# Two MLPs behind a Fourier transform on one core: VectorE's passes over a group of weights in another order and in other stages

## The chip, the core and the metric

The kernel runs on one core of a Trainium2 chip. The metric is device time in microseconds (us) of one execution; the kernel before took 1014.62 us (median of 3 runs, 1012.75 to 1015.59). One further execution was profiled: it took 1011.64 us, and its trace spans 1009.5 us from the first instruction to the last.

## The reference

```python
X = np.fft.fft(x, axis=1); X = np.fft.fft(X, axis=2); x = X.real      # x: 2 x 3008 x 256
x = x.reshape(6016, 256)
h = x @ w_in;   r = np.maximum(h, 0.0); g = r * r;                    x = g @ w_out     # d_ff 2048
h = x @ w2_in;  g = h * (1.0 / (1.0 + np.exp(-1.702 * h)));           out = g @ w2_out  # d_ff 2048
```

The four weight matrices are float64. The kernel gets them as 32-bit words (low word, high word) and makes fp32 numbers of them itself.

## The kernel before, in words

**Two parts.** In the first part (to about 505 us of the trace) the core transforms x, runs the first MLP and, between its steps, prepares all the weights. In the second part it runs the second MLP. The change touches the first part alone.

**Steps.** The first MLP runs in 128 steps (the loop at L701), each for one of 8 blocks of up to 378 columns and one of 16 groups of 128 features. In a step TensorE (PE) does 6 matmuls into the two halves of a PSUM pair (`front1`, L468 to L470; the pool `psa` holds two pairs) and, for the step that lies four back, 12 matmuls into accumulators (`back`, L483, pool `psb`). VectorE (DVE) makes `p` (L727) from the first half of the pair and the two parts of `h` (L729, L730) from the second half: only then is the pair free for the next `front1` but one. ScalarE (ACT) does Relu, Square and a rounded copy `gh` (L736, L737, L739), GpSimd (POOL) the rest `gl` = h - gh (L76, called from L744). In the steps of the set `SV` VectorE does Relu and Square in one pass (L734), in those of `VSTEPS` it does `gl` too. When a block of accumulators is done, ScalarE and VectorE copy one half of it each to SBUF (L596).

**A group of weights.** There are 16 groups, named (MLP, in or out, number). Each is a tile of 128 x 2048 words. `narrow` (L162) makes 128 x 1024 fp32 numbers of it in six passes: *abs* on ScalarE (L169); *low*, the low word times a constant, on ScalarE (L172, L180) for the keys in the set `RA` and on VectorE (L182) for the others; and on VectorE *clamp* (L173, needs abs), *shift* (L174, needs clamp), *merge* (L183, needs low and the raw words) and *sum* (L185, needs shift and merge). Then `widen` or `widen_in` splits the numbers into a rounded part (ScalarE, L208, L254) and a rest (POOL or VectorE).

**Where the passes stand.** Groups (0,0,0) and (0,1,0) are prepared before and in the first steps. For the other 14 `staged` (L214) says how many items of the generator each step takes: with the key in `RA` 2, 2, 2 (abs and low; clamp and shift; merge and sum), else 1, 3, 2 (abs; clamp, shift and low; merge and sum). Six of them belong to the first MLP (all with low on ScalarE), the eight of the second MLP follow from step 55 on. `background` (L573) takes the items at the end of a step, and from step 18 on they are not issued before the step's last `h` and `gh` (L752, L753). Within these bounds the compiler's scheduler sets the final order on each engine; an engine runs its instructions in that order and waits where the next one is not ready.

Of the kernel before, what the change touches and what calls it, by code (L numbers as in the profile page):

```python
# [12 lines left out]
AF = mybir.ActivationFunctionType  # L13
ALU = mybir.AluOpType
# [13 lines left out]
TOP = float(np.array(0x47EFFFFE, np.uint32).view(np.float32))  # L28
LEAST = float(np.array(0x38000000, np.uint32).view(np.float32))
# [14 lines left out]

LOW = {(0, 0, 0): "V", (0, 0, 1): "V", (0, 0, 2): "G", (0, 0, 3): "G", (0, 1, 0): "G", (0, 1, 1): "G", (0, 1, 2): "G", (0, 1, 3): "V", (1, 0, 0): "G", (1, 0, 1): "G", (1, 0, 2): "G", (1, 0, 3): "G", (1, 1, 0): "G", (1, 1, 1): "G", (1, 1, 2): "G", (1, 1, 3): "V"}
VSTEPS = {44, 45, 50, 58, 61, 72, 75, 82, 93, 96, 107, 110}
RA = {(0, 0, 0), (0, 0, 1), (0, 0, 2), (0, 0, 3), (0, 1, 1), (0, 1, 2), (0, 1, 3), (1, 0, 1)}
EOG = {1, 2, 3}
SV = {49, 51, 59, 60, 66, 73, 74, 79, 80, 94, 95, 101, 108, 109, 115}
LOWE = {(0, 0): "V", (0, 1): "G", (0, 2): "V", (0, 3): "V", (1, 0): "V", (1, 1): "G", (1, 2): "G", (1, 3): "V"}  # L50
# [13 lines left out]
def spectral_two_mlps_kernel(  # L64
# [5 lines left out]
    V, A, G, T = nc.vector, nc.scalar, nc.gpsimd, nc.tensor  # L70

    def f32(ap):
        return ap.bitcast(F32)
# [88 lines left out]
    def narrow(raw, ue, key=None):  # L162

        r = raw.rearrange("p (n w) -> p n w", w=2)
        lw, hw = r[:, :, 0], r[:, :, 1]
        u = ue[:, 0]
        uu, eu = u.bitcast(U32), ue[:, 1].bitcast(U32)

        yield lambda: A.activation(out=u, in_=f32(hw), func=AF.Abs)  # L169
        early = key in RA and key != (0, 0, 0)  # L170
        if early:
            yield lambda: A.activation(out=eu, in_=lw, func=AF.Copy, scale=2.0 ** -29)  # L172
        yield lambda: V.tensor_scalar(out=u, in0=u, scalar1=LEAST, scalar2=TOP, op0=ALU.max, op1=ALU.min)  # L173
        yield lambda: V.tensor_scalar(out=uu, in0=uu, scalar1=3, scalar2=0x3FFFFFF8,  # L174
                                      op0=ALU.logical_shift_left, op1=ALU.bitwise_and)

        if early:
            pass
        elif key in RA:
            yield lambda: A.activation(out=eu, in_=lw, func=AF.Copy, scale=2.0 ** -29)  # L180
        else:
            yield lambda: V.tensor_scalar(out=eu, in0=lw, scalar1=2.0 ** -29, scalar2=None, op0=ALU.mult)  # L182
        yield lambda: V.scalar_tensor_tensor(out=eu, in0=hw, scalar=0xC0000000, in1=eu,  # L183
                                             op0=ALU.bitwise_and, op1=ALU.bitwise_or)
        yield lambda: V.tensor_tensor(out=uu, in0=uu, in1=eu, op=ALU.add)  # L185

    def temp(pool, tag="xt"):
# [4 lines left out]
    def widen(mlp, kind, g, temps, dest, then=None, tag="xt"):  # L192
        low = G if LOW[mlp, kind, g] == "G" else V
        raw = raws.pop((mlp, kind, g))
        ue = temp(temps, tag)
        yield from narrow(raw, ue, (mlp, kind, g))
        if then:
            then()
        w = dest.tile([P, 2, 1024], F32R, tag="w", name="w")
        o = ue[:, 0]  # L200
        if (mlp, kind) == (0, 0):

            o = ue[:, 1]
            a, c = ue[:, 0, 0:512], ue[:, 0, 512:1024]
            yield lambda: (G if g in EOG else V).tensor_tensor(out=o[:, 0:512], in0=a, in1=c, op=ALU.add)
            yield lambda: V.scalar_tensor_tensor(out=o[:, 512:1024], in0=a, scalar=mask, in1=c,
                                                 op0=ALU.mult, op1=ALU.subtract)
        yield lambda: A.copy(w[:, 0], o)  # L208
        yield lambda: sub(low, w[:, 1], o, w[:, 0])
        if mlp and (kind, g) in PARKED:  # L210
            park((mlp, kind, g), w)
        weights[mlp, kind, g] = w

    def staged(key, gen):  # L214

        mlp, kind, _ = key
        first = (2, 2, 2) if key in RA else (1, 3, 2)
        for k in first + ((1,) if kind else (4, 1, 2) if mlp else (2, 1)):
            yield lambda: run(gen, k)
        yield lambda: run(gen)  # L220
# [271 lines left out]
    def run(gen, n=1 << 30):  # L492
        for _ in range(n):
            item = next(gen, None)
            if item is None:
                return False
            item()
        return True
# [35 lines left out]
    def small_w():  # L534
        yield from narrow(w1n_raw, w1n_t)
# [7 lines left out]
    def at(name, job):  # L543
        i, rate, end = PLAN[name]
        plan.setdefault(i, []).append((name, rate, job))
        if end is not None:
# [4 lines left out]
    at("odd0", lambda: odd_k(0, xp, "x2", 36))  # L551
    at("conv", lambda: chain(*(
        staged((0, k, g), widen(0, k, g, xp, (winp, wq)[k], tag=("t", "x0")[k],
                                then=(lambda k=k, g=g: load_w(0, k, g + 1)) if g < 3 else None))
        for g in (1, 2, 3) for k in range(2))))
# [145 lines left out]
    for i in range(n):  # L701
# [19 lines left out]
        elif done:  # L721
# [6 lines left out]
                               in1=ps[:, 0, 0:wd], op0=ALU.mult, op1=ALU.add)  # L728
# [76 lines left out]
    with tc.manual_schedule():  # L805
        for u in range(units + 2):
# [41 lines left out]
            if here:  # L848
                if p == 7 and j < BLKS - 1:
                    run(stage_a(j + 1))  # L850
                if rest is not None and not run(rest, 3 if j else (0, 2, 2, 4, 4, 4, 4, 4)[p]):
# [8 lines left out]
                                in1=cd[:, :, 0:wd], op=ALU.add)  # L860
# [155 lines left out]
```

## Time and profile before

| | |
|---|---|
| runs | 1014.62 us median (1012.75 to 1015.59) |
| profiled execution | 1011.64 us, span 1009.5 us |
| TensorE busy | 974.7 us (97%) |
| VectorE busy | 817.7 us (81%) |
| ScalarE busy | 609.9 us (60%) |
| GpSimd busy | 366.7 us (36%) |

Busy time says how much an engine had to do, not what it waited for. For that one reads the waits (who was idle until whom) and, around one group of weights, the instructions in order of time on the engines that wait.

### The profile page before, as it was taken

How to read it: one execution, taken by the hardware profiler on the slowest of the kernel's cores; microseconds unless marked ns; L12 is line 12 of the kernel's file. 1: busy time of each engine (PE TensorE's matmuls, PEld its weight loads, DVE VectorE, ACT ScalarE, POOL GpSimd, SP SyncE). 2: the span in 40 equal slices, each digit the busy share in tenths (PEclk: the TensorE clock that was granted, in tenths of full speed). 3: DMA queues.
4: the chain of work that ended last, by engine and by line, in shares of the span. 5: the costliest groups of instructions: out<-in, count | busy, mean ns of one | idle time of the engine just before them, and what ended most of it. 6: DMA issues, size and time to landing. Idle time of an engine off the chain costs nothing.

```text
span 1009.5 us, 14240 instructions
## 1 busy us (share of the span) xinstructions
PE 974.7 (97%) x5582; PEld 943.8 (93%) x5582; DVE 817.7 (81%) x1089; ACT 609.9 (60%) x758; POOL 366.7 (36%) x219
## 2 busy tenths in 40 slices
PE   8889989999999998999899999999999999999998
PEld 8579988999988897998899999999999999999997
DVE  7996888886898688895679888888888788888874
ACT  2588877866766676778645554545545445554443
POOL 2367687544768357778413302002020020200000
PEclk9999999999999999999999999999999999999999
DMA  7641221300332021201631100000100000000000
GB/s 293 213 148 44 84 103 43 104 31 25 115 118 112 32 84 65 81 1 62 218 103 59 65 1 31 31 32 31 31 1 32 31 32 31 1 31 1 32 1 31
DMA packets 22914, 65.22 MB, mean 65 GB/s; under 512 B 1856, under 2 KB 14272, under 8 KB 19648
## 3 DMA queue, kind: packets, MB, share of 16 engines
q1 hardware_dynamic: 22848, 64.32, 17.9%
q8 instruction: 43, 0.70, 0.3%
q14 instruction: 23, 0.19, 0.1%
HBM read 43.13 MB, written 21.19 MB: 64 GB/s over the span
## 4 chain that ended last, share of the span: by engine, by line
PE 69%; DVE 15%; ACT 7%; issue 5%; POOL 3%; DMA 1%; SPq 0%; DVEq 0%; ACTq 0%; POOLq 0%
PE psb L796 25%; PE psc L780 23%; PE psb L483 12%; PE psa L367 2%; ACT h L736 2%; PE psa L468 2%; ACT h L737 2%; DVE p L727 2%; PE psa L470 2%; DVE h L729 2%; PE psa L469 2%; DVE h L730 2%; POOL gl L76 1%; ACT gh L739 1%; DVE gl L76 1%
## 5 line engine op out<-in xcount | busy, mean ns | idle before, releaser
L76 POOL TENSOR_TENSOR gl<-h,gh 128x752 fp32r<-128x752 f32 (+1 forms) x116 | 224.9, 1944 | 139.2 <-ACT gh L739 108.6
L483 PE MATMUL psb<-gh,w 128*128 128x376 f32 (+1 forms) x1024 | 240.4, 338 | 2.4 <-ACT o L596 1.4
L796 PE MATMUL psb<-gh,w 128*128 128x376 f32 (+1 forms) x1024 | 237.7, 334 | 0.0
L483 PEld LDWEIGHTS psb<-gh,w 128*128 128x128 f32 x1024 | 183.6, 190 | 4.3 <-ACT o L596 2.0
L796 PEld LDWEIGHTS psb<-gh,w 128*128 128x128 f32 x1024 | 182.9, 188 | 0.0
L736 ACT ACTIVATE h<-h 128x752 f32<-128x752 f32 (+1 forms) x113 | 93.9, 832 | 74.5 <-DVE h L730 73.4
L861 ACT ACTIVATE g<-c 128x1128 f32<-128x1128 f32 (+1 forms) x64 | 73.7, 1152 | 98.9 <-DVE c L859 98.9
L483 PE MATMUL psb<-gl,w 128*128 128x376 f32 (+1 forms) x512 | 131.3, 337 | 2.0 <-POOL gl L76 2.0
L796 PE MATMUL psb<-gl,w 128*128 128x376 f32 (+1 forms) x512 | 129.9, 335 | 0.4 <-DVE gl L76 0.3
L739 ACT CAST gh<-h 128x752 fp32r<-128x752 f32 (+1 forms) x128 | 105.0, 822 | 22.6 <-DVE h L734 17.2
L630 POOL TENSOR_TENSOR ue<-raw 128x376 f32<-128x376 f32 (+1 forms) x16 | 19.4, 1235 | 270.5 <-DVE ya L76 270.4
L76 DVE TENSOR_TENSOR gl<-g,gh 128x1504 fp32r<-128x1504 f32 (+1 forms) x64 | 113.5, 1773 | 1.6 <-ACT gh L841 1.6
L841 ACT CAST gh<-g 128x1504 fp32r<-128x1504 f32 (+1 forms) x64 | 93.0, 1454 | 33.8 <-DVE g L832 33.8
L468 PE MATMUL psa<-eo,w 128*128 128x376 f32 (+1 forms) x256 | 89.2, 349 | 13.6 <-DVE h L730 8.2
L727 DVE SCALAR_TENSOR_TENSOR p<-n,w1n_t,psa 128x376 f32<-128x376 f32 (+1 forms) x128 | 76.2, 599 | 31.8 <-PE psa L470 31.7
L737 ACT ACTIVATE h<-h 128x752 f32<-128x752 f32 (+1 forms) x113 | 94.0, 834 | 3.0
L483 PEld LDWEIGHTS psb<-gl,w 128*128 128x128 f32 x512 | 93.4, 190 | 2.4 <-POOL gl L76 2.3
L796 PEld LDWEIGHTS psb<-gl,w 128*128 128x128 f32 x512 | 92.1, 188 | 1.0 <-DVE gl L76 1.0
L832 DVE TENSOR_TENSOR g<-g,c 128x1128 f32<-128x1128 f32 (+1 forms) x64 | 89.5, 1399 | 1.2 <-ACT g L861 1.2
L858 DVE TENSOR_TENSOR g<-g,psc 128x376 f32<-128x376 f32 (+1 forms) x64 | 35.0, 546 | 67.7 <-ACT g L857 67.7
L469 PE MATMUL psa<-eo,w 128*128 128x376 f32 (+1 forms) x256 | 85.9, 336 | 0.0
L470 PE MATMUL psa<-eo,w 128*128 128x376 f32 (+1 forms) x256 | 85.5, 335 | 0.0
(139 smaller groups left out, 1619.9 us busy)
## 6 DMA issues: line engine op xcount, KB each, us to landing
ydram<-o SPq DMA_DIRECT2D x18, 376.0 KB, 2.8
xt<-in_x SPq DMA_DIRECT2D x5, 1024.0 KB, 7.2
cst<-in_dfts SPq DMA_DIRECT2D x8, 570.0 KB, 5.6
raw<-ydram SPq DMA_DIRECT2D x6, 752.0 KB, 4.7
out<-o SPq DMA_DIRECT2D x11, 376.0 KB, 3.1
raw<-in_w1i SPq DMA_DIRECT2D x4, 1024.0 KB, 4.9
raw<-in_w1o SPq DMA_DIRECT2D x4, 1024.0 KB, 6.2
raw<-in_w2i SPq DMA_DIRECT2D x4, 1024.0 KB, 4.9
```

The lines of the kernel that those rows point to most:

```text
L76: eng.tensor_tensor(out=o, in0=a, in1=f32(b), op=ALU.subtract)
L468: T.matmul(o, lhsT=w[:, 0, fs], rhs=t[:, par, 0, 0:wd], start=True, stop=False)
L469: T.matmul(o, lhsT=w[:, 0, fs], rhs=t[:, par, 1, 0:wd], start=False, stop=False)
L470: T.matmul(o, lhsT=w[:, 1, fs], rhs=t[:, par, 0, 0:wd], start=False, stop=True)
L483: T.matmul(acc[j][ec][:, s, 0:wd], lhsT=w[:, hl, e0:e0 + P], rhs=(gh, gl)[gi][:, s, 0:wd], start=(first and hl == 0 and gi == 0), stop=(la ...
L727: V.scalar_tensor_tensor(out=p[:, 0:wd], in0=e128[blocks[j]][:, 0:wd], scalar=w1n_t[:, 0, f:f + 1], in1=ps[:, 0, 0:wd], op0=ALU.mult, op1= ...
L736: A.activation(out=hv, in_=hv, func=AF.Relu)
L737: A.activation(out=hv, in_=hv, func=AF.Square)
L739: last_a = A.copy(gh[:, :, 0:wd], hv)
L780: T.matmul(bank, lhsT=w[:, hl, slot * P:(slot + 1) * P], rhs=t[:, yl, i], start=(first and hl == 0 and yl == 0), stop=(hl == 1), skip_grou ...
L796: T.matmul(o[:, s, 0:wd], lhsT=w[:, hl, e0:e0 + P], rhs=g[:, 2 * i + s, 0:wd], start=(f == 0 and hl == 0 and g is gh), stop=(f == 15 and h ...
L841: A.copy(gh[:, :, 0:pw], g[:, :, 0:pw])
```

## The change

The order of the passes and the stages change; no pass gets another size.

- Keys not in `RA` (and not (0,1,0)): the first stage is now abs, low, merge; the second clamp and shift; the third sum (3, 2, 1 for 1, 3, 2). VectorE's passes begin one step earlier.
- Keys in `RA`, except (0,0,0): still 2, 2, 2, but merge stands in the second stage and shift in the third.
- (0,0,0), (0,1,0) and the small array of weights keep their order (the set `FIRST`).
- (1,0,1) leaves `RA`: its low moves from ScalarE to VectorE.

```diff
-RA = {(0, 0, 0), (0, 0, 1), (0, 0, 2), (0, 0, 3), (0, 1, 1), (0, 1, 2), (0, 1, 3), (1, 0, 1)}
+RA = {(0, 0, 0), (0, 0, 1), (0, 0, 2), (0, 0, 3), (0, 1, 1), (0, 1, 2), (0, 1, 3)}
+FIRST = {(0, 0, 0), (0, 1, 0), None}
...
+        def clamp():
+            V.tensor_scalar(out=u, in0=u, scalar1=LEAST, scalar2=TOP, op0=ALU.max, op1=ALU.min)
+
+        def shift():
+            V.tensor_scalar(out=uu, in0=uu, scalar1=3, scalar2=0x3FFFFFF8,
+                            op0=ALU.logical_shift_left, op1=ALU.bitwise_and)
+
+
+        def low():
+            if key in RA:
+                A.activation(out=eu, in_=lw, func=AF.Copy, scale=2.0 ** -29)
+            else:
+                V.tensor_scalar(out=eu, in0=lw, scalar1=2.0 ** -29, scalar2=None, op0=ALU.mult)
+
+        def merge():
+            V.scalar_tensor_tensor(out=eu, in0=hw, scalar=0xC0000000, in1=eu, op0=ALU.bitwise_and, op1=ALU.bitwise_or)
+
         yield lambda: A.activation(out=u, in_=f32(hw), func=AF.Abs)
...
+        if key in FIRST:
+            yield from (clamp, shift, low, merge)
         elif key in RA:
...
+            yield from (low, clamp, merge, shift)
         else:
...
+            yield from (low, merge, clamp, shift)
         yield lambda: V.tensor_tensor(out=uu, in0=uu, in1=eu, op=ALU.add)
...
-        first = (2, 2, 2) if key in RA else (1, 3, 2)
+        first = (2, 2, 2) if key in RA else (3, 2, 1)
```

In the rows of the changed kernel line numbers are larger: clamp is L171, shift L174, low L182 (ScalarE: L180), merge L185, sum L194, and `p` and `h` are L736, L738 and L739. The names `ue` and `raw` are the numbers in work and the words of a group, `psa` halves of a PSUM pair.

VectorE's order around group (1,0,0), before:

```order
L727 SCALAR_TENSOR_TENSOR p_3648<-n_2301,w1n_t_125,psa_3627 128x376
L729 TENSOR_TENSOR h_3647<-p_3648,psa_3628 128x376
L730 TENSOR_TENSOR h_3647<-p_3648,psa_3628 128x376
L182 TENSOR_SCALAR ue_3625<-raw_2978 128x1024
L727 SCALAR_TENSOR_TENSOR p_3682<-n_2301,w1n_t_125,psa_3661 128x376
L173 TENSOR_SCALAR ue_3625<-ue_3625 128x1024
L729 TENSOR_TENSOR h_3681<-p_3682,psa_3662 128x376
L174 TENSOR_SCALAR ue_3625<-ue_3625 128x1024
L730 TENSOR_TENSOR h_3681<-p_3682,psa_3662 128x376
L183 SCALAR_TENSOR_TENSOR ue_3625<-raw_2978,ue_3625 128x1024
L727 SCALAR_TENSOR_TENSOR p_3715<-n_2301,w1n_t_125,psa_3694 128x376
L185 ISA ue_3625<-ue_3625 128x2048
```

The same engine and the same steps in the changed kernel:

```order
L182 TENSOR_SCALAR ue_3625<-raw_2978 128x1024
L736 SCALAR_TENSOR_TENSOR p_3650<-n_2301,w1n_t_125,psa_3629 128x376
L185 SCALAR_TENSOR_TENSOR ue_3625<-raw_2978,ue_3625 128x1024
L738 TENSOR_TENSOR h_3649<-p_3650,psa_3630 128x376
L739 TENSOR_TENSOR h_3649<-p_3650,psa_3630 128x376
L736 SCALAR_TENSOR_TENSOR p_3683<-n_2301,w1n_t_125,psa_3662 128x376
L171 TENSOR_SCALAR ue_3625<-ue_3625 128x1024
L738 TENSOR_TENSOR h_3682<-p_3683,psa_3663 128x376
L174 TENSOR_SCALAR ue_3625<-ue_3625 128x1024
L739 TENSOR_TENSOR h_3682<-p_3683,psa_3663 128x376
L194 ISA ue_3625<-ue_3625 128x2048
L736 SCALAR_TENSOR_TENSOR p_3715<-n_2301,w1n_t_125,psa_3694 128x376
```

Low and merge moved a step up, clamp and shift kept their step and sum stands alone behind the second `h` pair; the other groups of the second MLP move in the same way.

VectorE's order around group (0,1,3), where a block of accumulators (`psb_1083`) is copied to SBUF, before:

```order
L727 SCALAR_TENSOR_TENSOR p_1338<-n_316,w1n_t_125,psa_1329 128x378
L173 TENSOR_SCALAR ue_1286<-ue_1286 128x1024
L727 SCALAR_TENSOR_TENSOR p_1385<-n_316,w1n_t_125,psa_1350 128x378
L596 COPY o_1318<-psb_1083 128x2x376
L174 TENSOR_SCALAR ue_1286<-ue_1286 128x1024
L729 TENSOR_TENSOR h_1337<-p_1338,psa_1330 128x378
```

The same place in the changed kernel:

```order
L605 COPY o_1318<-psb_1083 128x2x376
L736 SCALAR_TENSOR_TENSOR p_1338<-n_316,w1n_t_125,psa_1329 128x378
L171 TENSOR_SCALAR ue_1286<-ue_1286 128x1024
L738 TENSOR_TENSOR h_1337<-p_1338,psa_1330 128x378
L185 SCALAR_TENSOR_TENSOR ue_1286<-raw_1050,ue_1286 128x1024
```

The copy of the accumulators now stands ahead of two `p` and of clamp.

TensorE's order at the same place, behind the `front1` matmuls into psa_1351, before:

```order
L468 MATMUL psa_1398<-eo_304,w_874 128x378
L469 MATMUL psa_1398<-eo_304,w_874 128x378
L470 MATMUL psa_1398<-eo_304,w_874 128x378
L468 MATMUL psa_1435<-eo_304,w_874 128x378
L483 MATMUL psb_1358<-gh_1215,w_729 128x378 x2
```

And in the changed kernel:

```order
L492 MATMUL psb_1358<-gh_1215,w_729 128x378 x2
L492 MATMUL psb_1358<-gl_1252,w_729 128x378 x2
L492 MATMUL psb_1358<-gh_1215,w_729 128x378 x2
L492 MATMUL psb_1359<-gh_1215,w_729 128x378 x2
L492 MATMUL psb_1359<-gl_1252,w_729 128x378 x2
```

Four matmuls of later steps, which stood ahead of the new accumulators, now stand behind them.

## Rows read from the trace of the kernel before

**Rows 1.** The page, busy time (share) and instructions by engine.

```profile
PE 974.7 (97%) x5582; PEld 943.8 (93%) x5582; DVE 817.7 (81%) x1089; ACT 609.9 (60%) x758; POOL 366.7 (36%) x219
```

**Rows 2.** Waits of TensorE, 250 to 460 us: total us, times, longest.

```profile
PE psa L468 <- DVE h L730: 7.8, 8, 2.5
PE psb L483 <- ACT o L596: 1.4, 1, 1.4
```

**Rows 3.** Waits of VectorE, 60 to 505 us.

```profile
DVE ue L173 <- ACT ue L169: 6.9, 6, 1.9
```

**Rows 4.** The five passes on VectorE, 60 to 505 us: ns min/median/max.

```profile
L182 DVE TENSOR_SCALAR ue<-raw x7: 685/687/2292, 246.7 to 444.7; 128x1024 uint32<-128x1024 uint32 x7
L173 DVE TENSOR_SCALAR ue<-ue x12: 680/1372/2311, 64.2 to 445.8; 128x1024 f32<-128x1024 f32 x12
L174 DVE TENSOR_SCALAR ue<-ue x12: 675/694/1849, 66.5 to 446.5; 128x1024 uint32<-128x1024 uint32 x12
L183 DVE SCALAR_TENSOR_TENSOR ue<-raw,ue x12: 1210/1426/2576, 68.1 to 448.8; 128x1024 uint32<-128x1024 uint32 x12
L185 DVE CUSTOM_DVE_ANT_0 ue<-ue x12: 1207/1214/2739, 69.7 to 450.8; 128x2048 uint16<-128x2048 uint16 x12
```

**Rows 5.** Order of time at group (1,0,1): start, length, engine, [idle before <- releaser].

```profile
414.31 0.60 DVE L727 SCALAR_TENSOR_TENSOR p<-n,w1n_t,psa 128x376 f32<-128x376 f32 x1 [0.95 <-PE psa L470]
417.43 0.61 DVE L727 SCALAR_TENSOR_TENSOR p<-n,w1n_t,psa 128x376 f32<-128x376 f32 x1 [1.37 <-PE psa L470]
```

**Rows 6.** Order of time at group (1,0,0), VectorE, GpSimd and TensorE.

```profile
372.52 1.43 DVE L173 TENSOR_SCALAR ue<-ue 128x1024 f32<-128x1024 f32 x1 [0.96 <-ACT ue L169]
375.07 1.81 POOL L76 TENSOR_TENSOR gl<-h,gh 128x752 fp32r<-128x752 f32 x1 [1.67 <-issue]
375.38 2.58 DVE L183 SCALAR_TENSOR_TENSOR ue<-raw,ue 128x1024 uint32<-128x1024 uint32 x1
378.25 1.81 POOL L76 TENSOR_TENSOR gl<-h,gh 128x752 fp32r<-128x752 f32 x1 [1.37 <-ACT gh L739]
378.40 2.74 DVE L185 CUSTOM_DVE_ANT_0 ue<-ue 128x2048 uint16<-128x2048 uint16 x1
382.11 0.44 PE L468 MATMUL psa<-eo,w 128*128 128x376 f32 x1 [2.48 <-DVE h L730]
```

**Rows 7.** Order of time at group (1,1,2).

```profile
270.57 1.82 POOL L76 TENSOR_TENSOR gl<-h,gh 128x752 fp32r<-128x752 f32 x1
275.06 1.39 DVE L173 TENSOR_SCALAR ue<-ue 128x1024 f32<-128x1024 f32 x1 [1.45 <-ACT ue L169]
277.61 1.82 POOL L76 TENSOR_TENSOR gl<-h,gh 128x756 fp32r<-128x756 f32 x1 [1.72 <-issue]
283.14 0.44 PE L468 MATMUL psa<-eo,w 128*128 128x378 f32 x1 [0.90 <-DVE h L730]
285.61 0.44 PE L468 MATMUL psa<-eo,w 128*128 128x378 f32 x1 [1.15 <-DVE h L730]
```

**Rows 8.** Order of time at group (1,1,0).

```profile
400.14 1.36 DVE L173 TENSOR_SCALAR ue<-ue 128x1024 f32<-128x1024 f32 x1 [1.46 <-ACT ue L169]
404.52 2.32 DVE L185 CUSTOM_DVE_ANT_0 ue<-ue 128x2048 uint16<-128x2048 uint16 x1
407.81 0.44 PE L468 MATMUL psa<-eo,w 128*128 128x376 f32 x1 [1.53 <-DVE h L730]
```

**Rows 9.** Order of time at group (0,1,3).

```profile
137.78 0.89 DVE L173 TENSOR_SCALAR ue<-ue 128x1024 f32<-128x1024 f32 x1 [1.93 <-ACT ue L169]
139.24 0.44 PE L468 MATMUL psa<-eo,w 128*128 128x378 f32 x1 [1.95 <-DVE p L727]
140.37 0.94 DVE L596 COPY o<-psb 128x752 f32<-128x752 f32 x1 [1.19 <-POOL gl L76]
141.46 0.83 PE L483 MATMUL psb<-gh,w 128*128 128x378 f32 x2 [0.63 <-DVE o L596]
```

**Rows 10.** Busy time by engine, granted clock of TensorE, DMA, 140 to 160 us.

```profile
140.00:160.00 20.00, 19.37 (x103) 19.08 (x102) 18.90 (x26) 15.53 (x21) 13.38 (x8) 0.91 0.42 144
```

More of the change, by code (lines that the diff above doesn't have):

```diff
@@ L167, in narrow @@
         uu, eu = u.bitcast(U32), ue[:, 1].bitcast(U32)
-        yield lambda: A.activation(out=u, in_=f32(hw), func=AF.Abs)
[L170 to L178, printed above, removed]
+        def clamp():
[10 more added lines that the diff above has]
+            V.scalar_tensor_tensor(out=eu, in0=hw, scalar=0xC0000000, in1=eu, op0=ALU.bitwise_and, op1=ALU.bitwise_or)
+        yield lambda: A.activation(out=u, in_=f32(hw), func=AF.Abs)
+        if key in FIRST:
+            yield from (clamp, shift, low, merge)
         elif key in RA:
-            yield lambda: A.activation(out=eu, in_=lw, func=AF.Copy, scale=2.0 ** -29)
+            yield from (low, clamp, merge, shift)
         else:
-            yield lambda: V.tensor_scalar(out=eu, in0=lw, scalar1=2.0 ** -29, scalar2=None, op0=ALU.mult)
-        yield lambda: V.scalar_tensor_tensor(out=eu, in0=hw, scalar=0xC0000000, in1=eu,
-                                             op0=ALU.bitwise_and, op1=ALU.bitwise_or)
+            yield from (low, merge, clamp, shift)
         yield lambda: V.tensor_tensor(out=uu, in0=uu, in1=eu, op=ALU.add)
```

## The prediction

> **What bounds the kernel now.** I read the page first: TensorE is busy for 97% of the span, VectorE for 81% [rows 1]. So a change to VectorE's order can give back only what TensorE waits for VectorE, and the waits come next. Between 250 and 460 us, where seven of the eight groups of the second MLP are prepared, TensorE waits 8 times and 7.8 us in all for an `h`, and 1.4 us for ScalarE's copy of accumulators [rows 2]. Then I asked what VectorE itself waits for between 60 and 505 us: for 6.9 us, in 6 places, it stands at clamp until ScalarE has made abs [rows 3]. Last I read the instructions in order of time around the groups where TensorE stops [rows 6 to 9]. There the reader is to see two things: the wait for abs ahead of clamp, and passes that take twice their shortest time when a `gl` of GpSimd is running.
>
> **How much VectorE may do in a step.** At 414.31 and 417.43 VectorE has caught up with TensorE; a step is then 3.12 us, of which it idles 1.37 [rows 5]. So about 1.4 us of passes fit into a step for nothing. The shortest times are 0.69 for low, 0.68 for clamp, 0.68 for shift, 1.21 for merge and 1.21 for sum [rows 4]. Before, groups with low on VectorE put 0 / 2.05 / 2.42 us into their three steps, which is 0.65 + 1.02 = 1.7 over the free time; the changed kernel puts 1.90 / 1.36 / 1.21, 0.5 over in the first step, most of it given back by the third. On paper that is 1.2 to 1.7 us less lateness a group, and abs has a step's time to be ready. But the lateness is not the wait: with two PSUM pairs TensorE stops only when VectorE is more than a step behind, and most groups never come so far. Hence I take the groups one by one.
>
> **(1,0,0)** costs TensorE 2.48 us [rows 6]. VectorE waits 0.96 for abs; then clamp takes 1.43, merge 2.58 and sum 2.74, that is 0.75 + 1.37 + 1.53 over their shortest times [rows 4, 6]. Merge ends at 377.96 and sum at 381.14, each 1.08 after a `gl` of GpSimd ends (376.88 and 380.06): they stood still until GpSimd was through. The new order takes away the 0.96 surely. The five passes still have to find gaps between GpSimd's operations of 1.81, one in each step, and sum is still the last of them. Bounds: all 2.48 goes, or nothing. Shifting the passes by a step should spare about one third of the 3.65 of standing still, some 0.5 net of where it is met again; 0.96 + 0.5 = 1.4 or 1.5; I take -1.4.
>
> **(1,1,2)** costs 0.90 + 1.15 = 2.05 [rows 7]. The 1.45 of waiting for abs goes, but low would now be issued, by my estimate, behind an `h` pair at about 271.3, in the middle of the `gl` that runs from 270.57 to 272.39, and stand still for about 1.1; and the sum, at about 278.8, meets the `gl` of 277.61 or its successor. The second stop comes from a pass of `SV` that lies between two `h` in both kernels. Bounds -2.05 and +0.5 (one more pass standing still than now); I take -0.6.
>
> **(1,1,0)** costs 1.53 [rows 8]: 1.46 of waiting for abs, and a sum of 2.32. The first goes, low and clamp are likely to meet a `gl`. Bounds -1.53 and +0.5; -1.0. The 1.4 for ScalarE's copy [rows 2] stays: abs is ahead of this copy in ScalarE's order both times.
>
> **(1,0,3) and (1,1,1)** share what is left, 7.8 - 2.05 - 2.48 - 1.53 = 1.7. Neither waits for abs: of the 6.9 us in 6 places [rows 3], 0.96 + 1.45 + 1.46 + 1.93 lie at the four groups of [rows 6 to 9], and the 1.1 left lies at (0,0,3) and (1,0,2). So only the spread helps, and the new pair low and merge delays an `h` of the step ahead. Bounds -1.7 and +1; -0.3.
>
> **(1,0,1)** gets a pass that it did not have on VectorE: low, 0.69 at its shortest and 2.29 at its longest [rows 4]; ScalarE loses the same pass. VectorE idles 0.95 and 1.37 in the two steps ahead [rows 5], which covers low and merge (1.90) if they are not stopped, and TensorE does not wait there now. Bounds 0 and +2; +0.4.
>
> **(0,1,3)** is the one place where TensorE's own order changes. Now VectorE stands 1.93 for abs, TensorE stops for 1.95, and 0.63 more for VectorE's copy of the accumulators, which waits for a `gl` until about 140.3 [rows 9]. In the new order this copy comes first on VectorE, ahead of two `p` and clamp, and can't end sooner, since the same `gl` holds its buffer: `p` and clamp, 0.6 + 0.9 + 0.6 done before it today, come after it, so VectorE leaves the place 1 to 2 us later. TensorE does not have the four `front1` matmuls to fill the time (4 x 0.17, 974.7 over 5582 [rows 1]); it does half of the new accumulators (six, about 1.0) and then waits until about 141.2. So one wait of some 3.4 stands in the place of 1.95 + 0.63 = 2.6 with 0.7 of work still to do, 0.2 won at the end of the wait. The half that it does early is done today as well. In 140 to 160 us the granted clock is 0.91 on the mean [rows 10], so part of that stretch ran at the lower level (1.2 GHz) behind these waits; a longer wait may lengthen it. Bounds -1.5 and +2.5; +0.4.
>
> **The rest.** The other five groups with low on ScalarE cause no wait of TensorE that I found; theirs goes from 0 / 1.36 / 2.42 to 0 / 1.89 / 1.89, the same over the free time; 0, hidden by the second PSUM pair, and up to +1 where clamp, still waiting for abs, now stands ahead of an `h`. (1,0,2) and (1,1,3) have no wait to lose. DMA: the raw words are free as soon as merge has run, a step earlier, which no one waits for. The second part has none of these passes.
>
> **Sum.** -1.4 - 0.6 - 1.0 - 0.3 + 0.4 + 0.4 = -2.5. Against the profiled execution, 1011.64, that is 1009.1; that one ran 3.0 under the median of the runs shown, so on their footing I predict 1014.6 - 2.5 = 1012.1.
>
> The Trainium skill, SBUF — State Buffer, section "Who interferes with whom", says that VectorE and GpSimd share a pair of ports under an exclusive lock, that a VectorE instruction in a 2-port mode or with two SBUF inputs takes it, and that the later of the two "fully blocks" until the other has ended. The trace agrees: merge and sum end 1.08 after GpSimd does [rows 6]. By that rule alone lying evenly is worth nothing where a pass falls on a `gl`, and this makes the second rival below.
>
> **Rivals.** First: the waits for an `h` go almost wholly, because each of them needs the last bit of lateness and every group loses 1.2 to 1.7. For it: abs and these very passes stand ahead of the three longest waits [rows 6 to 8]. Against it: the amount of passes is the same and sum stays in its step. It gives 2.48 + 2.05 + 1.53 + half of 1.7 = 6.9 less, with the two costs above 6.1 less: 1008.5.
>
> Second, the other side: low and merge, now issued directly behind an `h` pair and often ahead of a `p` and `h`, meet the running `gl` and stand still, so that VectorE enters clamp's step later than today. The price of one is up to 1.5 (2.74 - 1.21, rows 4 and 6). It decides once VectorE is already a step behind, so in (1,1,2), (1,0,0), (1,1,0) and (1,1,1): 4 x 1.5 = 6.0 against the waits for abs that go, 1.45 + 0.96 + 1.46 = 3.9; +2.1. With (1,0,1) at its worst +2.0 this gives +4.1: 1018.7; for it speaks that low has been stopped to 2.29 and merge to 2.58 already [rows 4], against it that GpSimd's `gl` comes with each step, so most collisions are only traded.
>
> Third: nothing visible. What is saved ahead of a group is met again at its `gl`, its `SV` pass or its copies, TensorE's waits move but keep their sum: 1014.6.
>
> **How the numbers follow.** Forecast (1010.9 to 1013.4) 0.42; first rival 0.23; third 0.19; second 0.16. A difference of 0.3%, 3.0 us, is about what a measurement of this kernel can tell from no change. Faster by more than that, under 1011.6: the first rival 0.23 and some two fifths of the forecast, 0.17; together 0.40. Slower, over 1017.7: 0.13 of the second. Same: the remaining 0.47. The range reaches from the first rival with a clock that stays up in (0,1,3), 1007.0, to a second rival that decides in three groups, 1016.8.
>
> **What would show it.** In the trace of the changed kernel: VectorE's wait for abs falls from 6.9 to about 2.5, left at groups with low on ScalarE alone; TensorE's wait for `h` in 250 to 460 us falls from 7.8 to about 4.5; at (0,1,3) one wait of 3 to 4 us for VectorE's copy; no wait of TensorE over 1 us at (1,0,1). I am wrong if the waits for `h` stay at 7 or more (then GpSimd's lock decides), if they fall under 2, or if (0,1,3) costs over 5.

## The result: 0.5% slower, and the profile after

The changed kernel takes 1018.87 us (median of 7 runs, 1016.65 to 1021.32), the kernel before beside it 1013.83 us; the ratio is 1.0053, 95% interval 1.0038 to 1.0067. I had forecast 1012.1 us, with a range up to 1016.8. The profiled execution took 1021.32 us, its span is 1019.4 us.

The page of the changed kernel, busy time by engine, answers to [rows 1]:

```profile
PE 986.7 (97%) x5582; PEld 954.0 (94%) x5582; DVE 820.2 (80%) x1090; ACT 610.4 (60%) x757; POOL 362.9 (36%) x219
```

VectorE has the same work (817.7 before). TensorE does the same 5582 matmuls in 12 us more; its mean granted clock was 0.984 in this execution and 0.996 in that of the kernel before, so part of the matmuls ran at the lower level.

TensorE's waits between 250 and 460 us, against [rows 2], and VectorE's wait for abs between 60 and 505 us, against [rows 3] (total us, times, longest):

```profile
PE psa L477 <- DVE p L736: 3.5, 4, 2.1
PE psa L477 <- DVE h L739: 2.3, 8, 0.3
```

```profile
DVE ue L171 <- ACT ue L187: 1.4, 3, 1.1
```

The wait for abs fell from 6.9 to 1.4 us, the wait for `h` from 7.8 to 2.3; but waits of 3.5 us for a `p`, which now stands behind low and merge, came in their place. The longest of them is at (1,1,0):

```profile
404.74 0.44 PE L477 MATMUL psa<-eo,w 128*128 128x376 f32 x1 [2.07 <-DVE p L736]
```

The ScalarE copy of [rows 2] (1.4 us at 400 us) is not gone either: TensorE waits for it a block later, 1.8 us at 462.

The five passes on VectorE, 60 to 505 us (ns min/median/max), against [rows 4]:

```profile
L171 DVE TENSOR_SCALAR ue<-ue x12: 678/804/2125, 63.7 to 451.4; 128x1024 f32<-128x1024 f32 x12
L185 DVE SCALAR_TENSOR_TENSOR ue<-raw,ue x12: 1210/1226/2850, 66.0 to 449.4; 128x1024 uint32<-128x1024 uint32 x12
L174 DVE TENSOR_SCALAR ue<-ue x12: 677/680/694, 68.0 to 453.3; 128x1024 uint32<-128x1024 uint32 x12
L194 DVE CUSTOM_DVE_ANT_0 ue<-ue x12: 1210/2228/2850, 69.1 to 454.8; 128x2048 uint16<-128x2048 uint16 x12
L182 DVE TENSOR_SCALAR ue<-raw x8: 686/1346/2156, 249.2 to 448.3; 128x1024 uint32<-128x1024 uint32 x8
```

Clamp and shift are short now (median 1372 to 804 and 694 to 680, the longest shift 1849 to 694), but sum takes 2228 where it took 1214, and low 1346 where it took 687. The standing still has moved from two passes to two others: the seven long sums all end about 1 us after a `gl` of GpSimd does.

The end of each block of accumulators gives marks for the comparison. VectorE's copies of three of them, the last one just behind the start of the second part, in the kernel before (start, length; `...` stands for rows left out):

```profile
222.07 0.94 DVE L596 COPY o<-psb 128x752 f32<-128x752 f32 x1
...
455.47 0.93 DVE L596 COPY o<-psb 128x752 f32<-128x752 f32 x1
513.86 0.93 DVE L802 COPY o<-psb 128x752 f32<-128x752 f32 x1
```

The changed kernel:

```profile
227.21 0.94 DVE L605 COPY o<-psb 128x752 f32<-128x752 f32 x1
...
461.26 0.93 DVE L605 COPY o<-psb 128x752 f32<-128x752 f32 x1
524.93 0.94 DVE L811 COPY o<-psb 128x752 f32<-128x752 f32 x1
```

From the first row to the second, where the second MLP's groups are prepared and where I had looked for the effect, it is 233.4 us before and 234.1 after. Yet TensorE waits 3.9 us less there: between 250 and 460 us 9.7 us before (7.8 + 1.4 [rows 2], and 0.5 in two short waits), 5.8 after. The stretch between these two copies (length; busy time of PE, PEld, VectorE, ScalarE, GpSimd; clock; DMA), before and after:

```profile
222.07:455.47 233.40, 223.76 (x1265) 211.70 (x1263) 192.60 (x276) 163.25 (x211) 150.15 (x92) 1.00 0.20 72
227.21:461.26 234.05, 227.61 (x1264) 214.50 (x1262) 194.11 (x277) 163.06 (x210) 146.19 (x92) 0.99 0.20 71
```

What the waits gave back went into the matmuls: TensorE is busy for 3.85 us more, with the same matmuls (1265 and 1264 records). Part of it may be the clock: the granted clock is 0.91 in 280 to 300 and in 400 to 420 us, in both traces of the changed kernel, and 1.00 in this trace of before. How much of the 3.85 us that makes was not separated.

In these two traces the loss lies on either side of the stretch: 5.1 us ahead of 227 us, and 5.3 us at the end of the first part (58.4 against 63.7). The second traces, below, make both smaller.

### The profile page after: what moved, and what is told of

Same layout as the page of the kernel before. It is cut to its first block, busy times and chain, and to the rows that moved or that the text cites. A ratio compares the mean times of both kernels' runs of the same rounds, so it can differ in the third digit from the quotient of the medians.

```text
span 1019.4 us, 14237 instructions
## 1 busy us (share of the span) xinstructions
PE 986.7 (97%) x5582; PEld 954.0 (94%) x5582; DVE 820.2 (80%) x1090; ACT 610.4 (60%) x757; POOL 362.9 (36%) x219
## 4 chain that ended last, share of the span: by engine, by line
PE 62%; DVE 12%; ACT 4%; issue 2%; POOL 0%; DVEq 0%; ACTq 0%; POOLq 0%
PE psb L805 25%; PE psc L789 23%; PE psb L492 9%; DVE p L736 2%; DVE h L738 2%; PE psa L376 2%; DVE h L739 2%; PE psa L477 1%; DVE ue L194 1%; DVE h L743 1%; PE psa L479 1%; PE psa L478 1%; ACT h L746 1%; ACT h L745 1%; DVE gl L77 1%
## 5 line engine op out<-in xcount | busy, mean ns | idle before, releaser
L77 POOL TENSOR_TENSOR gl<-h,gh 128x752 fp32r<-128x752 f32 (+1 forms) x116 | 221.6, 1918 | 151.1 <-ACT gh L748 118.1
L492 PEld LDWEIGHTS psb<-gh,w 128*128 128x128 f32 x1024 | 187.6, 194 | 6.0 <-DVE o L605 3.4
L805 PEld LDWEIGHTS psb<-gh,w 128*128 128x128 f32 x1024 | 182.9, 188 | 0.0
L77 DVE TENSOR_TENSOR gl<-g,gh 128x1504 fp32r<-128x1504 f32 (+1 forms) x64 | 111.4, 1740 | 1.6 <-ACT gh L850 1.6
L477 PE MATMUL psa<-eo,w 128*128 128x376 f32 (+1 forms) x256 | 90.0, 352 | 11.2 <-DVE h L739 4.8
L736 DVE SCALAR_TENSOR_TENSOR p<-n,w1n_t,psa 128x376 f32<-128x376 f32 (+1 forms) x128 | 76.2, 599 | 28.2 <-PE psa L479 28.1
L492 PEld LDWEIGHTS psb<-gl,w 128*128 128x128 f32 x512 | 95.6, 194 | 0.4 <-POOL gl L77 0.4
L805 PEld LDWEIGHTS psb<-gl,w 128*128 128x128 f32 x512 | 92.1, 188 | 1.0 <-DVE gl L77 1.0
L738 DVE TENSOR_TENSOR h<-p,psa 128x376 f32<-128x376 f32 (+1 forms) x128 | 69.7, 544 | 21.1 <-POOL gl L77 8.2
L478 PE MATMUL psa<-eo,w 128*128 128x376 f32 (+1 forms) x256 | 86.3, 338 | 0.0
```

The costliest lines, as they stand in the source:

```text
L77: eng.tensor_tensor(out=o, in0=a, in1=f32(b), op=ALU.subtract)
L477: T.matmul(o, lhsT=w[:, 0, fs], rhs=t[:, par, 0, 0:wd], start=True, stop=False)
L478: T.matmul(o, lhsT=w[:, 0, fs], rhs=t[:, par, 1, 0:wd], start=False, stop=False)
L492: T.matmul(acc[j][ec][:, s, 0:wd], lhsT=w[:, hl, e0:e0 + P], rhs=(gh, gl)[gi][:, s, 0:wd], start=(first and hl == 0 and gi == 0), stop=(la ...
L736: V.scalar_tensor_tensor(out=p[:, 0:wd], in0=e128[blocks[j]][:, 0:wd], scalar=w1n_t[:, 0, f:f + 1], in1=ps[:, 0, 0:wd], op0=ALU.mult, op1= ...
L738: V.tensor_tensor(out=h[:, 0, 0:wd], in0=p[:, 0:wd], in1=ps[:, 1, 0:wd], op=ALU.add)
```

## The experiments

The table has the median of each kernel, its difference from the median of the kernel before in the same comparison, and the ratio with its 95% interval. The ratio differs from the quotient of the medians by up to 0.1% (1 us), so a difference of medians is known no better than that. Three kernels were traced once more: before (1016.04 us), the changed kernel (1021.93) and ra_no_012 (1013.39).

| kernel | us | difference | ratio, 95% |
|---|---|---|---|
| w2_only | 1013.79 | 0.0 | 0.9998 (0.9982 to 1.0013) |
| w2_and_101 | 1014.23 | +0.5 | 1.0009 (0.9993 to 1.0025) |
| ra_only | 1018.83 | +5.1 | 1.0046 (1.0031 to 1.0062) |
| old_012 | 1016.71 | +3.0 | 1.0031 (1.0017 to 1.0046) |
| only_012 | 1015.36 | +1.5 | 1.0010 (0.9995 to 1.0024) |
| ra_no_012 | 1017.00 | +3.2 | 1.0023 (1.0009 to 1.0038) |
| only_101 | 1014.84 | +1.5 | 1.0012 (1.0000 to 1.0023) |
| mlp1_no_012 | 1013.43 | +0.1 | 1.0005 (0.9993 to 1.0017) |
| new_001 | 1016.91 | +3.1 | 1.0020 (1.0002 to 1.0037) |
| w2_222 | 1019.66 | +6.0 | 1.0057 (1.0039 to 1.0074) |
| nyq_before | 1013.42 | -0.3 | 0.9989 (0.9975 to 1.0003) |
| after_yb | 1016.04 | +2.7 | 1.0031 (1.0019 to 1.0042) |
| before_yb | 1012.47 | -1.0 | 0.9989 (0.9978 to 1.0000) |
| before_nyq_yb | 1011.98 | -1.4 | 0.9985 (0.9974 to 0.9996) |
| w2_nyq_yb | 1011.23 | -2.2 | 0.9978 (0.9965 to 0.9991) |

**Which part of the change.** *w2_only* is the changed kernel with both edits on `RA` undone, *w2_and_101* with the second alone:

```diff
-RA = {..., (0, 1, 3)}
+RA = {..., (0, 1, 3), (1, 0, 1)}
-            yield from (low, clamp, merge, shift)
+            yield from (low, clamp, shift, merge)
```

*ra_only* keeps that order line, has (1,0,1) in `RA`, and undoes the staging:

```diff
-            yield from (low, merge, clamp, shift)
+            yield from (clamp, shift, low, merge)
-        first = (2, 2, 2) if key in RA else (3, 2, 1)
+        first = (2, 2, 2) if key in RA else (1, 3, 2)
```

> Only the groups of the second MLP are staged 3, 2, 1; the groups with low on ScalarE keep their old order, (1,0,1) too. Theory 1 (the time is lost at the first MLP's groups, where the copy of the accumulators at (0,1,3) now comes first and TensorE waits once for long): within 2 us of the kernel before, since the waits for h that go (about 4 us less between 250 and 460) are mostly met again. Theory 2 (low and merge of the second MLP's groups meet GpSimd): 3 to 5 us slower than before. Theory 3 (the waits keep their sum and what is lost is the clock, which falls after them more often): slower by half of the time that the granted clock is low beyond the kernel before's.

> The changed kernel, but with the old order (shift ahead of merge) in all groups with low on ScalarE; the second MLP's groups are staged 3, 2, 1 and (1,0,1) has low on VectorE. Theory 1: 4 to 5 us faster than the changed kernel, about as before. Theory 2: as the changed kernel, 5 us slower than before. Theory 3: by its low clock, as in the run with the second MLP's groups alone.

> Only merge and shift change places in the groups with low on ScalarE ((1,0,1) is still one of them); the second MLP's groups keep 1, 3, 2. Theory 1: 4 to 5 us slower than before, with the long wait for the copy at (0,1,3). Theory 2: within 1 us of before. Theory 3: slower by half of the additional time at the low clock, wherever that lies.

The staging by itself gives nothing and loses nothing that the interval can tell (-1.8 to +1.3 us); merge ahead of shift in the groups with low on ScalarE loses 5.1 us by itself. ra_only turns (1,0,1) too, which the change does not. The change's own order edit is what lies between w2_and_101 and the changed kernel: 1.0009 to 1.0053, about 4.5 us, with intervals that do not overlap. So by edits the change is 0.0 for the staging, 0.5 for (1,0,1) (not beyond its interval) and 4.5 for the order of six groups of the first MLP. Theory 2 falls; theory 3, the clock, is not excluded as a part of it. w2_only does gain where I forecast it, and gives it back at the end of the first part. Its copies at the same three places:

```profile
225.75 0.94 DVE L605 COPY o<-psb 128x752 f32<-128x752 f32 x1
...
457.43 0.93 DVE L605 COPY o<-psb 128x752 f32<-128x752 f32 x1
519.56 0.93 DVE L811 COPY o<-psb 128x752 f32<-128x752 f32 x1
```

231.7 us in the middle (233.4 before), then 62.1 (58.4 before). Of the 1.7 us won, 1.4 is the wait for ScalarE's copy, which has only moved behind the second row.

**Which group.** *old_012* is the changed kernel, but (0,1,2) keeps shift ahead of merge; *only_012* the kernel before with (0,1,2) alone reordered; *ra_no_012*, *mlp1_no_012* and *only_101* are ra_only with the new order in a part of the groups; *new_001* is w2_and_101 with the new order in (0,0,1) alone. The line of old_012 and ra_no_012:

```diff
-            yield from (low, clamp, merge, shift)
+            yield from (low, clamp, *((shift, merge) if key == (0, 1, 2) else (merge, shift)))
```

> The changed kernel, but group (0,1,2) alone with shift ahead of merge: by that alone the scheduler gives TensorE, and the copy of the accumulators at (0,1,3), the order of the kernel before again. Theory 1: 3 to 5 us faster than the changed kernel. Theory 2: no difference from the changed kernel (under 1 us). Theory 3: a difference only if the low clock of 125 to 205 us goes with it, about 3 us.

> The kernel before, with merge ahead of shift in group (0,1,2) alone; by that the scheduler turns the copy of the accumulators at (0,1,3) and TensorE's four matmuls there into the order of the changed kernel. Theory 1 (this turned order is the whole loss): 4 to 5 us slower than before. Theory 2 (it is a part of it, as taking it back gave 2.2 us, and the rest lies in the other groups with low on ScalarE): 2 to 3 us slower.

> Merge ahead of shift in all groups with low on ScalarE but (0,1,2); the second MLP's groups as before, TensorE's order as before. Theory 1: within 1 us of before, or up to 2 us faster since TensorE's wait at 51 us gets shorter. Theory 2: 2.5 to 3 us slower than before.

> The kernel before with merge ahead of shift in (0,0,1), (0,0,2), (0,0,3), (0,1,1) and (0,1,3), not in (0,1,2) and (1,0,1). If the first MLP's groups carry the loss of 2 to 3 us: as slow as that kernel; if (1,0,1) does: within 1 us of before.

> The kernel before with merge ahead of shift in group (1,0,1) alone. The kernel without (0,1,2) but with the other groups with low on ScalarE reordered lost 2 to 3 us, and its traces differ from before's only behind 380 us. If (1,0,1) carries that loss: 2 to 3 us slower than before. If the first MLP's groups carry it: within 1 us of before.

> The second MLP's groups staged 3, 2, 1, (1,0,1) with low on VectorE, and of the groups with low on ScalarE (0,0,1) alone with merge ahead of shift, so that merge runs before the h pair and TensorE's wait at 51 us (2.5 us before, 0.3 in the changed kernel) gets shorter; TensorE's order as before. Theory 1: 1 to 2 us faster than the kernel before, the sum of this wait and of what the second MLP's groups give. Theory 2: 0 to 3 us slower, if the order of (0,0,1) is where the rest of the loss comes from.

The copy at (0,1,3) that comes first there is made so by the order of *another* group, (0,1,2): old_012 gives TensorE the old order and 2.2 us (1.0053 to 1.0031, with intervals that overlap a little; ra_only to ra_no_012, the same step without the staging, is 1.8). Alone it costs 1.5 us, an amount that its interval does not tell from nothing, so theory 1 is a part at most. (1,0,1) alone (only_101) costs 1.5 more, at the edge of its interval, the other five groups of the first MLP nothing that shows. These parts make 3.1 of ra_only's 5.1; each is known to some 1.5 us, and whether the rest is error or comes of their combination stays open. The same question stands in the changed kernel: old_012 differs from w2_and_101 by the new order of these five groups alone and is 2.5 us slower, where mlp1_no_012 has the same five without the staging and loses 0.1; the two intervals overlap. new_001 is a miss: the wait at 51 us stayed at 1.97 us, and its 3.1 us loss (by the ratio 2.0, just beyond its interval) is not explained by (0,0,1), since mlp1_no_012 has the same edit and does not lose.

TensorE's wait at (0,1,3) in only_012, and the stretch of [rows 10] in it:

```profile
141.73 1.00 PE L492 MATMUL psb<-gh,w 128*128 128x378 f32 x2 [3.87 <-DVE o L605]
```

```profile
140.00:160.00 20.00, 18.27 (x90) 18.27 (x91) 17.39 (x27) 13.82 (x18) 12.41 (x7) 0.83 0.37 125
```

One wait of 3.87 us in the place of 1.95 + 0.63 [rows 9], as forecast; behind it the granted clock of the stretch is 0.83, not 0.91, so twice as much of it ran at 1.2 GHz, and the pair of matmuls behind the wait takes 1.00 where it took 0.83 [rows 9]. This clock is not firm: the second trace of before has 1.00 in 140 to 160 us, and both traces of the changed kernel have 0.91.

**Two traces of one program.** *before_2*, *after_2* and *ra_no_012_2* are unchanged kernels, traced again.

> The kernel before once more, for a second trace of it: its first one was at 1011.64 us 2 us faster than the median of its runs and had a mean granted clock of 0.996 where most of its runs have 0.990. If the difference between the two shown traces is the clock's, this one shows as much low clock as the changed kernel's trace and waits about as long in all; if not, the clock stays near 0.996.

> Another trace of the changed kernel, whose first one was of its slowest run. What belongs to the change must show again: the wait of 2.8 us for the copy at (0,1,3) with low clock behind it, waits of about 8 us in all between 225 and 480 us, 3.6 us for u at the end of the first part. What doesn't show again (the low clock at 290, 406 and 464) is this execution's.

> Another trace of the kernel with merge ahead of shift in the groups with low on ScalarE but (0,1,2): its first trace was of its fastest run. If its loss of 2 to 3 us in the median lies at a place, a wait appears in this trace that the two traces of before do not have; if it is the clock alone, the waits are those of its first trace and the low clock is longer.

TensorE's first wait for `eo` and the busy times of 165 to 190 us (PE, PEld, VectorE, ScalarE, GpSimd, clock, DMA), the first trace of before:

```profile
171.71 0.44 PE L431 MATMUL psa<-eo,sel_t 128*128 128x376 f32 x1 [1.06 <-ACT eo L375]
```

```profile
165.00:190.00 25.00, 21.85 (x129) 21.03 (x128) 21.00 (x32) 20.14 (x27) 14.56 (x11) 1.00 0.22 74
```

The second trace of the same program:

```profile
170.52 0.44 PE L431 MATMUL psa<-eo,sel_t 128*128 128x376 f32 x1 [2.34 <-ACT eo L375]
```

```profile
165.00:190.00 25.00, 21.54 (x113) 20.89 (x112) 18.21 (x27) 17.97 (x24) 13.21 (x9) 0.86 0.22 73
```

The granted clock is 1.00 in one and 0.86 in the other, and 113 matmul records stand where 129 stood. So the trace on which I rested the forecast is not the typical one: its mean clock is 0.996, while over all timed runs of before the median is 0.991. Over the changed kernel's it is 0.990, and on the mean 0.988 against 0.991. By an estimate (0.001 of 1014 us is 1.0 us of TensorE at full clock) that is 1 to 3 of the 5.0 us lost, so the clock alone does not separate the two kernels, and a part of it may.

The three copies, in the second trace of before (the first of them is shown in the last section) and of the changed kernel:

```profile
458.25 0.93 DVE L596 COPY o<-psb 128x752 f32<-128x752 f32 x1
...
518.21 0.94 DVE L802 COPY o<-psb 128x752 f32<-128x752 f32 x1
```

```profile
225.66 0.94 DVE L605 COPY o<-psb 128x752 f32<-128x752 f32 x1
...
459.68 0.93 DVE L605 COPY o<-psb 128x752 f32<-128x752 f32 x1
523.35 0.94 DVE L811 COPY o<-psb 128x752 f32<-128x752 f32 x1
```

The middle is the same again (233.8 and 234.0; TensorE busy for 224.4 and 227.7). The first mark is at 224.50 and 225.66, so of the 5.1 us ahead of it the second pair shows 1.2. The end of the first part takes 60.0 in the second trace of before, 1.6 more than in the first, and 63.7 in both of the changed kernel: 3.7 of the 5.3 us are left there.

after_2 repeats the wait at (0,1,3) (2.84) and the end of the first part to 0.01 us, the low clock at 290 and 406 us too, and not that at 464; so of my three guesses for chance one was right. ra_no_012_2 shows the same waits as its first trace; both executions (1012.91 and 1013.39) lie over 3 us under its median, and no place for its loss was found in them.

*nyq_before* takes the wait for `eo` away, by one idle step ahead of the two matmuls:

```diff
         yield lambda: split_eo(b, 3, e3)
-        yield from [lambda: None] * b
+        yield from [lambda: None] * (b + 1)
```

> The kernel before with the two sel_t matmuls of the fourth block (L431, L432) issued one step later, behind another step's front1 and back; nothing else changes on TensorE or VectorE. It takes away the wait for eo at 171 us (1.06 + 1.11 in the first trace, 2.34 + 1.12 in the second) without touching a weight group. If the low clock that follows this wait in some executions is a cost of its own (the second trace of before loses 3.6 us between 139 and 224 us against the first, by the same program): 3 to 5 us faster than before, less spread between its runs, and a granted clock of 1.00 between 160 and 190. If only the wait counts: 1 to 2 us faster. If VectorE and ScalarE set the end of the first part anyway: no difference.

It gives 0.11%, within its interval; the wait there shrank to 0.42, but one of 2.35 for a `p` came at 183 us, with low clock behind it. The larger gain that I had expected did not come.

**Two passes in each stage.** *w2_222* is w2_only with stages of equal number (with abs, two passes each):

```diff
-        first = (2, 2, 2) if key in RA else (3, 2, 1)
+        first = (2, 2, 2)
```

> The kernel before with the second MLP's groups staged 2, 2, 2 in the order low; merge, clamp; shift, sum: no pass waits for abs, as in 3, 2, 1, but merge no longer stands ahead of a p in the first step. If lying evenly helps once merge is out of the first step: 1 to 3 us faster than before. If the waits that go are met again (theory 3, and what 3, 2, 1 alone showed): within 1 us of before.

Both expectations miss: it is 6.0 us slower. Its waits of TensorE, 250 to 460 us:

```profile
PE psa L477 <- DVE h L739: 6.5, 11, 2.1
PE psa L477 <- DVE p L736: 3.0, 5, 1.4
PE psb L492 <- DVE o L605: 0.8, 1, 0.8
PE psb L492 <- ACT o L605: 0.2, 1, 0.2
```

10.5 us, more than before's 9.7. By VectorE's shortest times its stages hold 0.69 / 1.89 / 1.89 us, where 3, 2, 1 has 1.90 / 1.36 / 1.21 and 1, 3, 2 has 0 / 2.05 / 2.42. So it lies more evenly than 1, 3, 2, which is 6.0 us faster, and 3, 2, 1, the most even, is as fast as 1, 3, 2: evenness is not what decides. What makes 2, 2, 2 the slowest was not found.

**The end of the first part.** At about 485 us VectorE makes two rests `yb` (128 x 378 each) for the second part. VectorE and GpSimd there, the kernel before (a row merges equal instructions, x5 is five `gl` without a gap):

```profile
473.78 8.83 POOL L76 TENSOR_TENSOR gl<-h,gh 128x752 fp32r<-128x752 f32 x5
...
481.32 1.70 DVE L76 TENSOR_TENSOR yb<-raw,yb 128x378 fp32r<-128x378 f32 x1
...
482.95 0.54 DVE L76 TENSOR_TENSOR yb<-ue,yb 128x378 fp32r<-128x378 f32 x1
```

The changed kernel:

```profile
480.83 11.07 POOL L77 TENSOR_TENSOR gl<-h,gh 128x752 fp32r<-128x752 f32 x6
...
486.92 3.31 DVE L77 TENSOR_TENSOR yb<-raw,yb 128x378 fp32r<-128x378 f32 x1
...
490.15 2.16 DVE L77 TENSOR_TENSOR yb<-ue,yb 128x378 fp32r<-128x378 f32 x1
```

w2_only:

```profile
476.99 11.37 POOL L77 TENSOR_TENSOR gl<-h,gh 128x752 fp32r<-128x752 f32 x6
...
483.07 1.49 DVE L77 TENSOR_TENSOR yb<-raw,yb 128x378 fp32r<-128x378 f32 x1
...
484.48 2.17 DVE L77 TENSOR_TENSOR yb<-ue,yb 128x378 fp32r<-128x378 f32 x1
```

In the changed kernel a pass of 0.54 takes 3.31 and 2.16, and the second ends 0.4 after GpSimd's six `gl` do (491.90). In the kernel before the first rest comes 1.3 us ahead of the end of GpSimd's run (482.61), and the second is free. Both traces of the changed kernel have it, 5.5 and 5.4 us in all; both of before have 2.2. The six `gl` alone do not make the difference: w2_only, old_012 and ra_only have six there too, with some 5 us left to run, and the rests take 3.6 to 3.7. VectorE then comes late with `p`, and TensorE stands at the start of the second part, in the changed kernel:

```profile
501.87 1.31 PE L789 MATMUL psc<-yb,w2i 128*128 128x378 f32 x6 [1.72 <-DVE p L736]
510.08 2.23 PE L789 MATMUL psc<-yc,w2i 128*128 128x378 f32 x5 [3.63 <-DVE u L845]
```

and in the kernel before:

```profile
501.00 0.79 PE L780 MATMUL psc<-yc,w2i 128*128 128x378 f32 x3 [2.23 <-DVE u L836]
502.24 1.31 PE L780 MATMUL psc<-yc,w2i 128*128 128x378 f32 x6 [0.45 <-DVE c L838]
```

5.35 us for 2.68. The Trainium skill, SBUF — State Buffer, section "Who interferes with whom", says that the later of two takers of the shared ports waits until the other has ended. The trace agrees, with the 0.4 us above; and in a run of `gl` without gaps VectorE can be kept out for longer than one of them lasts (3.31 - 0.54 = 2.8 us, a single `gl` 1.8).

*after_yb*, *before_yb* give these two rests to GpSimd, where they take 1.0 and 0.9; nothing else changes its order. *before_nyq_yb* has nyq_before's step too, and *w2_nyq_yb* both and the staging of w2_only:

```diff
-            yield lambda: sub(V, o[:, 1, i], x, o[:, 0, i])
+            yield lambda: sub(low or V, o[:, 1, i], x, o[:, 0, i])
...
-        yield from split(o, ((0, yr[j][:, 0, 0, 0:wd]), (1, ts[j][:, 2, 0:wd])))
+        yield from split(o, ((0, yr[j][:, 0, 0, 0:wd]), (1, ts[j][:, 2, 0:wd])), G if j == 0 else V)
```

> The changed kernel with the two yb rests of the first block of the second part (128 x 378 each, at about 485 us) on GpSimd in place of VectorE; the order of everything else is the same. In both traces of the changed kernel they take 5.44 us on VectorE, in those of before 2.24, since a gl of GpSimd runs across them, and TensorE then waits 1.7 us for p. If this is a piece of the loss: 2 to 3 us faster than the changed kernel, without the wait for p at 500 us. If TensorE's wait for u behind it takes up what is saved: within 1 us of the changed kernel.

> The kernel before with the two yb rests on GpSimd alone. In the changed kernel this gave 2.8 us, where they take 5.44 us on VectorE; here they take 2.24. If the gain is their time beyond what both kernels share, it is under 1 us here; if they cost TensorE whatever their length, it is 2 us or more.

> The kernel before with two repairs: the sel_t matmuls one step later (alone 1.1 us faster, within its interval of no change), and the two yb rests on GpSimd. If both waits cost what their stretches show: 2 to 4 us faster than before, and the fastest of all kernels here. If the end of the first part is set by ScalarE's chain to u: 1 us faster, by the first alone.

> Both repairs (sel_t matmuls one step later, the two yb rests on GpSimd) and the staging 3, 2, 1 of the second MLP's groups, with the old order of all groups with low on ScalarE. By the traces the staging gains about 2 us between 225 and 460 us and gives them back at the end of the first part, where the yb rests took 3.66 in place of 2.24. If the yb rests were all that gave it back: 1 to 2 us faster than the two repairs alone, 2.5 to 3.5 us faster than before. If the end of the first part gives it back anyway: as fast as the two repairs alone, 1.5 us faster than before.

The changed kernel gets faster by it, 2.8 us by the medians of two comparisons and 2.2 by the ratios (1.0053 to 1.0031). The copies of after_yb at the end of the first part:

```profile
460.81 0.94 DVE L605 COPY o<-psb 128x752 f32<-128x752 f32 x1
518.84 0.94 DVE L811 COPY o<-psb 128x752 f32<-128x752 f32 x1
```

58.0 us in the place of 63.7. The kernel before gains 1.0, at the edge of its interval, so that of the 2.2 to 2.8 us 1 to 2 are what the change brought. With both repairs, the staging 3, 2, 1 makes the fastest kernel of all: 1011.23 us, 0.22% under before (interval 0.09 to 0.35%) and 7.6 under the changed kernel. That the staging itself gives 0.7 us of this is not shown, its interval and that of before_nyq_yb overlap.

## Why the prediction was wrong, step by step

- **The waits for abs and `h`: right in sum, not in place.** About 2.5 was forecast to be left of abs's 6.9, 1.4 was; of `h`'s 7.8, 4.5, and it is 5.8 with the waits for `p`. But (1,0,0), from which 1.4 was to go, has 0.5 left of its 2.48, and (1,1,0), from which 1.0 was to go, has a longer one, 2.07 for a `p` in place of 1.53, so that the sum came near is luck in part. None of my signs of being wrong appeared, so they looked at the wrong places.
- **The staging, -1.4 - 0.6 - 1.0 - 0.3 = -3.3, measured 0.0 (w2_only): a step that failed.** I took a wait that goes for time won and let it count to the end ("The second part has none of these passes"). In the changed kernel TensorE waits 3.9 us less between 250 and 460 us, and is busy for 3.85 more in the stretch around it. In w2_only 1.7 us are won there and lost again at the end of the first part, 62.1 against 58.4 and 60.0 in the two traces of before. There are none of these passes between 460 and 515 us either, but VectorE, ScalarE and GpSimd still have to bring `yb`, `ya` and `yc` there, and TensorE waits for them: 2.7 us in the trace of before, 5.35 after.
- **"The other five groups ... 0, hidden by the second PSUM pair": the step that failed by the most.** The order of these five and of (0,1,3), +0.4 in the sum, measures about +4.5 (w2_and_101 to the changed kernel). 2.2 of it is the order of (0,1,2), one of the five, which acts at (0,1,3). The rest comes with the order of the other groups beside the staging (w2_and_101 to old_012), and how is open.
- **(0,1,3): the mechanism right, the size too small.** One wait of 2.8 to 3.9 us came, as worked out. I took +0.4 of bounds up to +2.5; it measures +1.5 (only_012, within its interval) to +2.2 (old_012). The lower clock behind the longer wait, which I had put into the bound, is there in only_012 and ra_only (0.83 in 140 to 160 us) and not in the changed kernel (0.91). I also took it for an effect of (0,1,3)'s own order; it is (0,1,2)'s.
- **(1,0,1) on VectorE: +0.4 forecast**, and w2_and_101 is 0.4 slower than w2_only; neither is beyond the intervals.
- **The base.** The forecast rests on one trace at 1011.64; a second trace of before, at 1016.04, has low clock at 165 to 190 us where the first has none. It was an error to treat all of TensorE's waits and clock in one execution as the program's.
- **The rivals.** The second one's number, 1018.7, is the nearest to the result, but that is luck: its mechanism and place are not what happened, since the staging that it is about measured 0.0. GpSimd's lock has a part in the loss (after_yb, 2.2 to 2.8 us), 100 us behind the place where I had put it.

Not settled: why the two rests take 5.4 us in both traces of the changed kernel, when old_012, whose order behind 150 us is the same and which has six `gl` there too, shows the 3.7 us of w2_only; what the new order of the five groups costs beside the staging; how much of the loss is the clock; and 2 us of ra_only. The repairs of (0,1,2) and of `yb` were not tried together.

## What to carry to other kernels

Follow a gain to the next place where the bounding engine waits for the others whatever it does (the end of a phase above all), and count only what passes through it. A wait that goes is time won only if the stretch around it gets shorter; measure it between two marks. Where two engines lock each other out, look at where in the other one's run of operations a pass lands, not at how evenly the passes lie. Where a scheduler sets the order, compare the whole order of both kernels: an edit of one group turned a wait at another. And take the waits and the clock from two executions before a term rests on them.

## What the runs showed of the hardware

In the same program TensorE's clock fell behind a wait in one trace and not in the other. Between 280 and 300 us the two traces of before show the same waits for `h` (0.90 and 1.15; 0.90 and 1.16), and a granted clock of 1.00 in the first and 0.91 in the second:

```profile
280.00:300.00 20.00, 17.94 (x102) 17.28 (x102) 18.14 (x25) 13.99 (x18) 14.44 (x7) 1.00 0.40 145
280.00:300.00 20.00, 17.94 (x94) 17.23 (x94) 16.66 (x25) 15.17 (x19) 14.82 (x8) 0.91 0.39 145
```

From copy to copy that cost little: 233.75 us (224.50 to 458.25) against 233.40. At 171 us, where the wait was longer in the second trace (2.34 for 1.06), it cost more. VectorE's copies on both sides, in the second trace of before:

```profile
139.15 0.94 DVE L596 COPY o<-psb 128x752 f32<-128x752 f32 x1 [1.18 <-POOL gl L76]
...
224.50 0.94 DVE L596 COPY o<-psb 128x752 f32<-128x752 f32 x1
```

85.35 us, against 222.07 - 140.37 = 81.70 in the first ([rows 9] and the first copy shown above): 3.65 us more, of which the longer wait itself is 1.3.
